# One decode step of attention plus a gated feed-forward: the score sum moved from VectorE trees to identity matmuls, and all loads moved to one queue of 4 MiB transfers

## The chip, the cores and the metric

The kernel runs on one core of one Trainium2 chip. The metric is the device time of one execution in microseconds; three runs of the kernel before took 1370.96 to 1371.06 us, with a median of 1371.04 us. One further execution was taken by the hardware profiler; its page and its trace are what the rows below come from.

## The reference

One token `x` (640 values) is normalised and goes through two branches whose results are added to it:

```python
def _A_ref(x, k_cache, v_cache, wq, wo):          # 32 heads, Sk = 32768 keys, Dh = 128
    q = (x @ wq).reshape(B, Sq, Hq, Dh).transpose(0, 2, 1, 3)
    scores = einsum("bhqd,bhkd->bhqk", q, k) * (Dh ** -0.5)
    p = softmax(scores, axis=-1)
    o = einsum("bhqk,bhkd->bhqd", p, v)
    return o.transpose(0, 2, 1, 3).reshape(B, Sq, Hq * Dh) @ wo

def _B_ref(x, w_gate, w_up, w_down):              # F = 1728
    return (silu(x @ w_gate) * (x @ w_up)) @ w_down

xn = _layernorm(x)
return x + _A_ref(xn, k_cache, v_cache, wq, wo) + _B_ref(xn, w_gate, w_up, w_down)
```

Everything is bf16. Each of the 32 heads has its own K and V of 32768 x 128 values, 8 MiB each, and each is read once: 536.9 MB of the 555.2 MB that the profiled execution moved. There is one query per head, so a key gives 128 products and one sum.

## The kernel before

**Layout.** A head's K is laid over the 128 partitions so that partition p holds keys 256p to 256p+255, each with its 128 values side by side. A score is therefore a product with the head's query (which `qb` holds, the same in all partitions) and a sum along the free axis. K and V are each cut into four chunks of 64 keys per partition (2 MiB) a head.

**Queues.** SyncE issues x, the five pieces of `wq`, then the 128 K chunks into a ring of four slots (`krings`), with the feed-forward weights after the second chunk and `wo` after the fourth. A K chunk is issued when VectorE has finished with the chunk that lay in its slot (line 510). ScalarE issues the 128 V chunks on its own queue into another ring of four slots (`vrings`), each when TensorE has finished with the chunk before it in that slot (line 403). The feed-forward weights lie in `vrings` at first, so V waits for the feed-forward part (line 405).

**VectorE, per K chunk (lines 352 to 378).** One product of 128x8192 elements in place (L361), then a tree of four in-place additions over halves of the head axis, 64, 32, 16 and 8 wide (L365), then a reduction of the last 8 (L368). Once per head follow the maximum (L343) and a reciprocal (L349).

**GpSimd** takes the maximum over the partitions (L387) and scales it (L390), and later sums the softmax denominators (L394). **ScalarE** takes the exponential (L424) and copies out the head's result (L414). **TensorE** multiplies V with the probabilities: per V chunk 64 matmuls with one column (L466), and per head two more with `wo` (L440).

**Start and end.** The feed-forward part runs near the start (L287, L328) and borrows VectorE between K chunks. The output is a row in one partition: two additions of 1x640 at the very end (L483, L485) and one store (L524).

## Time and profile before

| what | value |
|---|---|
| median of 3 runs | 1371.04 us |
| span of the profiled execution | 1367.0 us (what lies around the span is not on the page; the median is 4.0 us above it) |
| VectorE busy | 1263.9 us, 92% |
| TensorE matmuls busy | 272.6 us, 20% |
| moved by DMA | 555.19 MB, 406 GB/s over the span |

In the profile, L361 is line 361 of the kernel; a group of instructions stands with its count, its busy time and the mean time of one. "DMA share" in the view by stretches is the time that packets took as a share of 16 DMA engines; since packets overlap a little, a full stretch shows 1.00 to 1.06. "PEclk" is the granted clock of TensorE as a share of full speed. Idle time stands with what ended it.

### The profile page before, as it was taken

To read this page: it belongs to the slowest core of one execution; us is meant where nothing else is said; L and a number is where in the kernel's file an instruction comes from. 1 tells how busy PE (TensorE), PEld (TensorE's weight loads), DVE (VectorE), ACT (ScalarE), POOL (GpSimd) and SP (SyncE) were. 2 spreads that over 40 slices of the span, in tenths; PEclk is the share of its full clock that TensorE was granted. 3 is DMA by queue.
4 is the path that set the end of the run, shared out by engine and by line. 5 is a ranking of instruction groups with operands and counts; after the bars stand their busy time and mean duration, and the time that the engine had idled before them with its cause. 6 is when DMAs were issued, how large, how long until landed. Compare 5 with 4: busy or idle time off the path is not lost.

```text
span 1367.0 us, 18528 instructions
## 1 busy us (share of the span) xinstructions
PE 272.6 (20%) x8474; PEld 240.2 (18%) x8474; DVE 1263.9 (92%) x859; ACT 31.9 (2%) x102; POOL 201.3 (15%) x100
## 2 busy tenths in 40 slices
PE   3320102222111222211122221112222111222222
PEld 1220102222101222210122221112222111222222
DVE  5907999999999999999999999999999999999994
ACT  0000000000000000000000000000000000000000
POOL 0000222111111211111121111111111111110120
PEclk9555555555555555555555555555555555555555
DMA  9999599999999999999999999999999999999994
GB/s 389 401 415 381 214 424 388 419 419 415 416 426 418 427 418 422 424 419 426 418 421 420 424 420 423 427 420 425 422 421 424 417 427 425 419 426 427 414 381 183
DMA packets 44850, 555.19 MB, mean 406 GB/s; under 512 B 4258, under 2 KB 10084, under 8 KB 11364
## 3 DMA queue, kind: packets, MB, share of 16 engines
q1 hardware_dynamic: 26340, 285.57, 50.4%
q10 hardware_dynamic: 18432, 268.44, 46.5%
q8 instruction: 66, 1.08, 0.3%
q14 instruction: 12, 0.10, 0.0%
HBM read 553.99 MB, written 0.00 MB: 405 GB/s over the span
## 4 chain that ended last, share of the span: by engine, by line
DVE 90%; another core or an unknown queue 3%; issue 2%; SPq 2%; DMA 1%; PE 1%; POOL 0%; ACT 0%; POOLq 0%
DVE krings L365 43%; DVE krings L361 40%; DVE sc L368 6%; DMA vrings<-in_B_w_down_dram 1%; SPq L499 1%; PE ps L466 1%; SPq L498 0%; DVE rzb L349 0%; PE ps L287 0%; SPq L494 0%; DVE pmax L343 0%; PE ps L440 0%; SPq L513 0%; DVE rows L483 0%
## 5 line engine op out<-in xcount | busy, mean ns | idle before, releaser
L365 DVE TENSOR_TENSOR krings<-krings 128x4096 bf16<-128x4096 bf16 (+3 forms) x512 | 592.9, 1158 | 17.5
L361 DVE TENSOR_TENSOR krings<-krings,qb 128x8192 bf16<-128x8192 bf16 x128 | 564.9, 4413 | 43.5 <-DMA krings<-in_A_k_cache_dram 43.5
L466 PE MATMUL ps<-P,vrings 128*128 128x1 bf16 x8192 | 229.5, 165 | 209.0 <-ACT P L424 105.5
L466 PEld LDWEIGHTS ps<-P,vrings 128*128 128x128 bf16 x8192 | 223.9, 104 | 228.4 <-ACT P L424 105.8
L387 POOL PARTITION_ALL_REDUCE gmaxb<-pmax x32 | 136.3, 4259 | 542.6 <-DVE pmax L343 542.6
L440 PE MATMUL ps<-wqo,ocol 128*1 128x320 bf16 x64 | 22.0, 449 | 850.7 <-ACT P L424 850.7
L440 PEld LDWEIGHTS ps<-wqo,ocol 128*1 128x1 bf16 x64 | 2.8, 81 | 853.6 <-ACT P L424 853.2
L368 DVE TENSOR_REDUCE sc<-krings 128x64 f32<-128x512 bf16 x128 | 87.8, 686 | 4.4
L394 POOL PARTITION_ALL_REDUCE zb<-rowsum x32 | 40.3, 1258 | 265.2 <-issue 265.2
L390 POOL TENSOR_SCALAR negb<-gmaxb 128x1 f32<-128x1 f32 x32 | 24.6, 767 | 351.4 <-issue 351.4
L424 ACT ACTIVATE P<-sc,negb 128x256 bf16<-128x256 f32 x32 | 16.3, 508 | 917.1 <-POOL negb L390 917.1
L349 DVE RECIPROCAL rzb<-zb 128x1 f32<-128x1 f32 x32 | 4.9, 153 | 14.4 <-POOL zb L394 14.4
L414 ACT ACTIVATE ocol<-ps,rzb 128x1 bf16<-128x1 f32 x32 | 8.4, 263 | 360.4 <-PE ps L466 360.4
L274 DVE CAST qb<-ps 128x512 bf16<-128x512 f32 x8 | 5.5, 692 | 11.9 <-PE ps L264 11.9
L343 DVE TENSOR_REDUCE pmax<-sc 128x1 f32<-128x256 f32 x32 | 13.4, 419 | 1.1
L264 PE MATMUL ps<-wqo,xnb 128*128 128x512 bf16 x40 | 10.1, 418 | 7.6 <-DMA wqo<-in_A_wq_dram 7.6
L287 PE MATMUL ps<-xncol,vrings 128*128 128x1 bf16 (+1 forms) x140 | 4.4, 168 | 16.7 <-DMA vrings<-in_B_w_down_dram 16.7
L287 PEld LDWEIGHTS ps<-xncol,vrings 128*128 128x128 bf16 (+1 forms) x140 | 4.3, 108 | 17.2 <-DMA vrings<-in_B_w_down_dram 17.2
L328 PE MATMUL ps<-vrings,hcol 128*1 128x320 bf16 (+1 forms) x28 | 6.4, 400 | 0.8 <-DVE hcol L307 0.8
L264 PEld LDWEIGHTS ps<-wqo,xnb 128*128 128x128 bf16 x40 | 4.2, 106 | 13.2 <-issue 9.5
L424 ACT ACTIVATION_READ_ACCUMULATOR P<-sc,negb 128x1 f32 x32 | 6.0, 187 | 0.0
L328 PEld LDWEIGHTS ps<-vrings,hcol 128*1 128x1 bf16 (+1 forms) x28 | 2.8, 104 | 4.4 <-issue 1.1
(31 smaller groups left out, 17.1 us busy)
## 6 DMA issues: line engine op xcount, KB each, us to landing
krings<-in_A_k_cache_dram SPq DMA_DIRECT2D x128, 2048.0 KB, 17.1
vrings<-in_A_v_cache_dram ACTq DMA_DIRECT2D x128, 2048.0 KB, 26.1
wqo<-in_A_wq_dram SPq DMA_DIRECT2D x5, 1024.0 KB, 9.0
wqo<-in_A_wo_dram SPq DMA_DIRECT2D x1, 5120.0 KB, 71.2
vrings<-in_B_w_gate_dram SPq DMA_DIRECT2D x1, 2160.0 KB, 26.4
vrings<-in_B_w_up_dram SPq DMA_DIRECT2D x1, 2160.0 KB, 31.1
vrings<-in_B_w_down_dram SPq DMA_DIRECT2D x1, 2080.0 KB, 31.7
vrings<-in_B_w_down_dram SPq DMA_DIRECT2D x1, 80.0 KB, 18.1
```

The costliest lines, as they stand in the source:

```text
L264: mm = t.matmul(QPS[b], lhsT=xnb[:, c, :], rhs=wq_v[:, c, b * QB:(b + 1) * QB], start=(c == 0), stop=(c == NC_D - 1))
L343: v1 = dve_max.inc(v.tensor_reduce(out=pmax[:, b % SR:b % SR + 1], in_=scs, axis=AX.X, op=ALU.max))
L361: dve_t.inc(v.tensor_tensor(out=kr, in0=kr, in1=qbh[:, None, :].to_broadcast([128, CKK, DH]), op=ALU.mult))
L365: dve_t.inc(v.tensor_tensor(out=kr[:, :, 0:w], in0=kr[:, :, 0:w], in1=kr[:, :, w:2 * w], op=ALU.add))
L368: v3 = dve_t.inc(v.tensor_reduce(out=scs[:, c * CKK:(c + 1) * CKK], in_=kr[:, :, 0:TREE[-1]], axis=AX.X, op=ALU.add))
L387: v1 = pool_g.inc(g.partition_all_reduce(gmaxb[:, s:s + 1], pmax[:, s:s + 1], channels=128, reduce_op=ReduceOp.max))
L390: v2 = pool_neg.inc(g.tensor_scalar(out=negb[:, s:s + 1], in0=gmaxb[:, s:s + 1], scalar1=-c_scale, scalar2=None, op0=ALU.mult))
L394: v3 = pool_z.inc(g.partition_all_reduce(zb[:, s:s + 1], rowsum[:, s:s + 1], channels=128, reduce_op=ReduceOp.add))
L424: v1 = act_exp.inc(a.activation(out=P[:, b % PR, :], in_=sc[:, b % SCR, :], func=ACTF.Exp, bias=negb[:, b % SR:b % SR + 1], scale=c_scale, ...
L440: mm = t.matmul(psR[0:1, b, 0:DBW], lhsT=ocol[:, h:h + 1], rhs=wo_v[:, h, b * DBW:(b + 1) * DBW], start=(h == 0), stop=(h == H - 1))
L466: mm = t.matmul(ob[:, 0:1], lhsT=ring[:, vslot, jj * DH:(jj + 1) * DH], rhs=P[:, pslot, j:j + 1], start=(j == 0), stop=(j == NJ - 1))
L499: c_ffn.inc(sp.dma_start(wd_sb[:, 0:FB - 1, :], B_w_down[0:(FB - 1) * 128, :].rearrange("(j p) n -> p j n", p=128)))
```

## The change

The kernel is written anew around the same reference; what matters for its time is this.

**Loads.** All loads go through SyncE's queue, in one order, into one ring of six slots of 4 MiB (128 keys per partition): `wq` first (it lies in slots 4 and 5), then K and V chunks of 4 MiB in turn, V one head behind K, then the feed-forward weights (two slots), `wo` (two slots) and the last head's V, whose last chunk comes in four pieces of 64, 32, 16 and 16 keys per partition. Each load waits until its slot's owner is used up: K until TensorE has summed it, V until TensorE has multiplied it.

**Scores.** VectorE still forms the product K*q in place, 128x8192 at a time, two per chunk. The tree is gone: TensorE adds the 128 products of a key with 16 matmuls of 512 columns against an identity matrix, each taking 8 of the 128 products of 64 keys and accumulating into one PSUM bank of 64x8; VectorE then reduces the last 8 out of PSUM. Four banks take turns.

**Order on TensorE.** Per K chunk: 32 identity matmuls, then the 128 matmuls of one V chunk of the head before. The feed-forward part, the products with `wo` for 31 heads and the last head's V come after all K chunks.

**Form of the rest.** x, the normalisation, the feed-forward result and the output lie over the partitions as columns (128x5), not as a row in one partition; the products with `wo` and `w_down` use the weights as the stationary operand with one moving column, 5 matmuls per head instead of 2. The query is copied out of PSUM by ScalarE instead of VectorE. Silu is computed with the exponential. The last head is copied out by VectorE.

The diff, cut to what the prediction speaks of:

```diff
-    CKK = 64 if NJ >= 64 else NJ
-    KR = 4
-    VR = 4
-    TREE = [64, 32, 16, 8]
+    CH = 128
+    HF = 64
+    G = 512 // HF
+    SLOTS = 6
+    NBK = 4
+    TAIL = [64, 32, 16, 16]
...
+    units += [("ffn",), ("wo",)]
+    units += [("v", H - 1, c) for c in range(NCH)]
...
+            @block.sync
+            def sp(e):
+                e.dma_start(xb[:, :], A_x[0, 0:1, :].rearrange("o (p c) -> (o p) c", c=NCD)).then_inc(s_x, 16)
+                e.dma_start(wq, A_wq.rearrange("(p c) n -> p (c n)", c=NCD)).then_inc(s_wq, 16)
...
+                for u in units:
+                    s = slot_of[u]
+                    for o in ([s, s + 1] if u[0] in ("ffn", "wo") else [s]):
+                        if o in owner:
+                            e.wait_ge(*owner.pop(o))
+                    if u[0] == "k":
+                        _, h, c = u
+                        e.dma_start(ring[:, s, :], kv_src(A_k_cache, h, c * CH, CH)).then_inc(s_slot[s], 16)
+                        owner[s] = (s_qk, NHF * (h * NCH + c + 1))
...
+                        e.dma_start(wo, A_wo.rearrange("(h d) n -> d h n", d=DH)).then_inc(s_wo, 16)
...
+                def scores(k):
+                    h, c = divmod(k, NCH)
+                    kv = ring[:, slot_of[("k", h, c)], :].rearrange("p (j d) -> p j d", d=DH)
+                    for i in range(NHF):
+                        n = k * NHF + i
+                        t.wait_ge(s_mul, n + 1)
+                        if n >= NBK:
+                            t.wait_ge(s_red, n - NBK + 1)
+                        ob = bank[n % NBK].rearrange("p (j e) -> p j e", e=G)
+                        for g in range(DH // G):
+                            mm = t.matmul(ob, lhsT=ident[:, :], rhs=kv[:, i * HF:(i + 1) * HF, g * G:(g + 1) * G],
+                                          start=(g == 0), stop=(g == DH // G - 1))
+                        mm.then_inc(s_qk, 1)
...
+                for k in range(NK):
+                    scores(k)
+                    h, c = divmod(k, NCH)
+                    if h >= 1:
+                        pv(h - 1, c)
...
-                    for w in TREE:
-                        v.wait_ge(dve_t.sem, dve_t.n)
-                        dve_t.inc(v.tensor_tensor(out=kr[:, :, 0:w], in0=kr[:, :, 0:w], in1=kr[:, :, w:2 * w],
-                                                  op=ALU.add))
...
+                    for i in range(NHF):
+                        kh = kv[:, i * HF:(i + 1) * HF, :]
+                        v.tensor_tensor(out=kh, in0=kh, in1=q[:, None, :].to_broadcast([128, HF, DH]),
+                                        op=ALU.mult).then_inc(s_mul, 1)
...
+                    for i in range(NHF):
+                        n = k * NHF + i
+                        v.wait_ge(s_qk, n + 1)
+                        j = c * CH + i * HF
+                        v.tensor_reduce(out=sc[:, h % SCR, j:j + HF],
+                                        in_=bank[n % NBK].rearrange("p (j e) -> p j e", e=G),
+                                        axis=AX.X, op=ALU.add).then_inc(s_red, 1)
...
+                v.wait_ge(s_att, 1)
+                v.tensor_tensor(out=outb[:, :], in0=xf[:, :], in1=acc, op=ALU.add).then_inc(s_fin, 1)
```

How the work stands on the engines: a row is a line of the respective kernel, its operation, what it writes and reads, the shape, and in brackets what it waits for. First VectorE, in the middle of the K stream. Before, two chunks of 64 keys (kd0, kd1 are the loads, dve_t VectorE's own last result):

```order
L361 TENSOR_TENSOR krings<-krings,qb 128x8192 [waits kd0]
L365 TENSOR_TENSOR krings<-krings 128x64x64 [waits dve_t]
L365 TENSOR_TENSOR krings<-krings 128x64x32 [waits dve_t]
L365 TENSOR_TENSOR krings<-krings 128x64x16 [waits dve_t]
L365 TENSOR_TENSOR krings<-krings 128x64x8 [waits dve_t]
L368 TENSOR_REDUCE sc<-krings 128x64 [waits dve_t]
L361 TENSOR_TENSOR krings<-krings,qb 128x8192 [waits kd1]
```

Now, one head of 256 keys, that is two chunks of 128 (slot2 and slot4 are the loads, qk the identity matmuls, z the softmax denominator of the head before):

```order
L385 TENSOR_TENSOR ring<-ring,qb 128x8192 [waits slot2,act_q]
L385 TENSOR_TENSOR ring<-ring,qb 128x8192
L393 TENSOR_REDUCE sc<-ps 128x64 [waits qk] x2
L385 TENSOR_TENSOR ring<-ring,qb 128x8192 [waits slot4,act_q]
L385 TENSOR_TENSOR ring<-ring,qb 128x8192
L393 TENSOR_REDUCE sc<-ps 128x64 [waits qk] x2
L400 TENSOR_REDUCE pmax<-sc 128x1 [waits red,gm]
L373 RECIPROCAL rzb<-zb 128x1 [waits z]
```

The four additions between a product and its reduction are gone, and between the products and the reductions VectorE now waits for TensorE. TensorE at the same place, before (vd0, vd1 are V loads):

```order
L440 MATMUL ps<-wqo,ocol 1x320 [waits c_wo,act_ov,act_exp]
L440 MATMUL ps<-wqo,ocol 1x320
L466 MATMUL ps<-P,vrings 128x1 [waits vd0]
L466 MATMUL ps<-P,vrings 128x1 x63
L466 MATMUL ps<-P,vrings 128x1 [waits vd1]
L466 MATMUL ps<-P,vrings 128x1 x63
```

and now (mul are VectorE's products, red its reductions, exp the exponential, ov the copy of a head's result):

```order
L241 MATMUL ps<-ring,ident 128x512 [waits red,mul]
L241 MATMUL ps<-ring,ident 128x512 x15
L241 MATMUL ps<-ring,ident 128x512 [waits red,mul]
L241 MATMUL ps<-ring,ident 128x512 x15
L263 MATMUL ps<-P,ring 128x1 [waits slot5,ov,exp]
L263 MATMUL ps<-P,ring 128x1 x127
L241 MATMUL ps<-ring,ident 128x512 [waits red,mul]
```

The 32 identity matmuls of a K chunk now stand ahead of each V chunk's 128 matmuls on the same engine, and the next chunk's identity matmuls behind them. Last, the end of SyncE's queue, which before held K chunks only and then the store:

```order
L166 DMA ring<-in_A_k_cache_dram 128x16384 [waits qk]
L176 DMA ring<-in_A_v_cache_dram 128x16384 [waits pv]
L179 DMA ring<-in_B_w_gate_dram 128x8640 [waits pv,qk]
L180 DMA ring<-in_B_w_up_dram 128x8640
L181 DMA ring<-in_B_w_down_dram 128x13x640
L183 DMA ring<-in_B_w_down_dram 64x640
L185 DMA ring<-in_A_wo_dram 128x32x640 [waits pv,qk]
L176 DMA ring<-in_A_v_cache_dram 128x16384 [waits qk]
L171 DMA ring<-in_A_v_cache_dram 128x8192 [waits pv]
L171 DMA ring<-in_A_v_cache_dram 128x4096
L171 DMA ring<-in_A_v_cache_dram 128x2048 x2
L187 DMA out_0_dram<-outb 128x5 [waits fin]
```

The feed-forward weights and `wo` moved from the start of the queue to a place behind the last K chunk, and the last head's V stands behind them.

More of the change, by code (lines that the diff above doesn't have):

```diff
@@ L90, in bass_parallel_sum__gqa_block_cached__swiglu_ffn__decode_kernel @@
-    for q in range(NVC):
-        _emit_v(q)
-    assert CKV == CKK, "V-in-K-slot staging needs equal chunk sizes"
-    LASTV_Q0 = (H - 1) * NCV
-    def v_buf(q):
-        return ("v", q % VR, None)
-    WO_POS = min(KR - 1, NKC - 1)
-    FFNW_POS = min(1, NKC - 1)
+    units = []
+    for h in range(H):
+        for c in range(NCH):
+            units.append(("k", h, c))
+            if h >= 1:
+                units.append(("v", h - 1, c))
+    units += [("ffn",), ("wo",)]
+    units += [("v", H - 1, c) for c in range(NCH)]
@@ L105, in sem @@
             return es.enter_context(nc.semaphore(name))
[L107 to L112 removed]
+        ring = sbt("ring", [128, SLOTS, CE], BF16)
+        qb = sbt("qb", [128, H * DH], BF16)
         sc = sbt("sc", [128, SCR, NJ], F32)
         P = sbt("P", [128, PR, NJ], BF16)
[L115 removed]
```

699 lines of the change are left out of this document (288 added, 411 removed).

## The prediction

> **What bounds the kernel now.** I read the page's shares and chain first, then who waited for whom, then the stretches of the span, then one chunk in order of time.
>
> ```profile
> span 1367.0 us, 18528 instructions
> PE 272.6 (20%) x8474; PEld 240.2 (18%) x8474; DVE 1263.9 (92%) x859; ACT 31.9 (2%) x102; POOL 201.3 (15%) x100
> DVE 90%; another core or an unknown queue 3%; issue 2%; SPq 2%; DMA 1%; PE 1%; POOL 0%; ACT 0%; POOLq 0%
> L365 DVE TENSOR_TENSOR krings<-krings 128x4096 bf16<-128x4096 bf16 (+3 forms) x512 | 592.9, 1158 | 17.5
> L361 DVE TENSOR_TENSOR krings<-krings,qb 128x8192 bf16<-128x8192 bf16 x128 | 564.9, 4413 | 43.5 <-DMA krings<-in_A_k_cache_dram 43.5
> L368 DVE TENSOR_REDUCE sc<-krings 128x64 f32<-128x512 bf16 x128 | 87.8, 686 | 4.4
> DMA packets 44850, 555.19 MB, mean 406 GB/s; under 512 B 4258, under 2 KB 10084, under 8 KB 11364
> SPq L513 <- DVE sc L368: 1196.7, 121, 31.2
> ```
>
> VectorE is busy for 92% of the span and makes up 90% of the chain that ended last. It waited for a K load once, for 43.5 us, while K's queue waited for VectorE 121 times. Two groups carry it: the product (564.9 us) and the tree (592.9 us). One chunk in order of time, with the head's end behind it:
>
> ```profile
> 1295.42 0.69 DVE L368 TENSOR_REDUCE sc<-krings 128x64 f32<-128x512 bf16 x1
> 1296.02 4.42 DVE L361 TENSOR_TENSOR krings<-krings,qb 128x8192 bf16<-128x8192 bf16 x1
> 1300.47 4.74 DVE L365 TENSOR_TENSOR krings<-krings 128x4096 bf16<-128x4096 bf16 x4
> 1305.24 0.69 DVE L368 TENSOR_REDUCE sc<-krings 128x64 f32<-128x512 bf16 x1
> 1305.96 0.42 DVE L343 TENSOR_REDUCE pmax<-sc 128x1 f32<-128x256 f32 x1
> 1306.37 4.41 DVE L361 TENSOR_TENSOR krings<-krings,qb 128x8192 bf16<-128x8192 bf16 x1
> ```
>
> From reduction to reduction a chunk takes 1305.24 - 1295.42 = 9.82 us, and a head's end adds (1306.37 - 1296.02) - 9.82 = 0.53. 128 x 9.82 + 32 x 0.53 = 1274 us, of a span of 1367. Per head VectorE needs 4 x 9.82 + 0.53 = 39.8 us for 16.78 MB of K and V, which is 421 GB/s. The second question is therefore how far the DMA engines could go:
>
> ```profile
> 0.00:5.00 5.00, 0.00 (x0) 0.00 (x0) 2.88 (x8) 1.28 (x1) 0.19 (x4) 1.00 0.50 184
> 10.00:15.00 5.00, 0.00 (x0) 0.00 (x0) 0.00 (x0) 0.00 (x0) 0.00 (x0) 1.00 1.02 431
> 15.00:20.00 5.00, 3.93 (x13) 1.53 (x14) 0.95 (x2) 0.00 (x0) 0.00 (x0) 1.00 1.01 433
> 25.00:30.00 5.00, 1.18 (x6) 0.33 (x4) 4.44 (x3) 0.00 (x0) 0.00 (x0) 0.90 1.02 417
> 50.00:60.00 10.00, 4.62 (x22) 1.91 (x20) 9.83 (x7) 1.28 (x1) 0.00 (x0) 0.84 1.02 372
> 140.00:160.00 20.00, 0.00 (x0) 0.00 (x0) 19.66 (x14) 0.00 (x0) 4.52 (x1) 0.50 0.55 210
> 180.00:200.00 20.00, 0.00 (x0) 0.00 (x0) 19.62 (x15) 0.00 (x0) 4.52 (x1) 0.50 1.01 429
> 210.00:215.00 5.00, 5.00 (x192) 5.00 (x192) 4.93 (x4) 0.00 (x0) 0.56 (x1) 0.50 0.50 170
> 200.00:1300.00 1100.00, 218.82 (x7224) 198.59 (x7224) 1080.20 (x718) 24.24 (x84) 176.26 (x83) 0.50 1.00 421
> 1340.00:1350.00 10.00, 0.00 (x0) 0.00 (x0) 6.05 (x8) 0.00 (x0) 0.37 (x1) 0.50 0.75 318
> 1350.00:1360.00 10.00, 5.07 (x168) 4.53 (x169) 0.00 (x0) 0.75 (x3) 0.26 (x1) 0.50 0.01 2
> ```
>
> The last three columns are TensorE's clock, DMA share and GB/s. Full stretches give 417 to 433; the average of 421 holds dips such as 210:215, when V's queue ran dry. So the two limits lie close together, and removing VectorE's can gain only what the DMA engines lost: the half-empty stretch around 140:160, the dips, and the last 20 us, in which almost nothing was loaded.
>
> **The change part by part.** *The tree leaves VectorE*: 592.9 us of busy time. What stays is 128 products of 4.41 (565 us), 128 reductions out of PSUM, and the heads' ends (17). The reduction's nearest rows are L368, 0.69 us for 512 elements from SBUF, and the copy of as many out of PSUM:
>
> ```profile
> L274 DVE CAST qb<-ps 128x512 bf16<-128x512 f32 x8 | 5.5, 692 | 11.9 <-PE ps L264 11.9
> 17.73 0.15 PEld L264 LDWEIGHTS ps<-wqo,xnb 128*128 128x128 bf16 x1 [0.28 <-issue]
> 18.16 0.15 PEld L264 LDWEIGHTS ps<-wqo,xnb 128*128 128x128 bf16 x1 [0.28 <-issue]
> 18.90 6.79 PEld L264 LDWEIGHTS ps<-wqo,xnb 128*128 128x128 bf16 x32 [0.16 <-issue]
> 48.17 6.45 PE L328 MATMUL ps<-vrings,hcol 128*1 128x320 bf16 x28 [0.84 <-DVE hcol L307]
> 608.09 5.28 PE L466 MATMUL ps<-P,vrings 128*128 128x1 bf16 x192
> ```
>
> Both say 0.69; 128 x 0.69 = 88. VectorE comes to 670 us of work and is no bound by itself.
>
> *TensorE gains 4096 identity matmuls of 512 columns.* The 512-column matmuls of the query start 0.43 us apart at first (17.73, 18.16) and then 6.79 / 32 = 0.212 us apart. The granted clock stood at 0.50 all through the one-column matmuls (200:1300) and rose to a mean of 0.84 in 50:60, around the 28 matmuls of 320 columns. So each chunk's identity matmuls should begin at 0.43 and reach 0.212 within some 3 us: about 7 x 0.43 + 25 x 0.212 = 8.3 us; bounds 6.8 (all fast) and 13.8 (all slow). The 128 V matmuls take 128 x 5.28 / 192 = 3.5 us, as before.
>
> *The new waits.* In a chunk VectorE waits for the matmuls and the next products queue behind that wait. Loop = first product 4.42 + matmuls + one reduction 0.69 + hops between engines about 0.3 + half a head's end 0.26 = 5.7 + 8.3 = 14.0 us, bounds 12.5 and 19.5. The second product hides under the first half's matmuls, the V matmuls under the next product (3.5 against 4.4). The loads that it must keep pace with are a K and a V chunk, 8.39 MB: 19.6 us at 428 GB/s. So VectorE should wait for loads about 5 us a chunk; even the slow bound only just fills that time.
>
> TensorE also waits for the exponential ahead of a head's first V chunk, with the next identity matmuls behind it. That chain is GpSimd's:
>
> ```profile
> 1323.06 0.51 ACT L424 ACTIVATE P<-sc,negb 128x256 bf16<-128x256 f32 x1 [25.10 <-POOL negb L390]
> 1346.29 0.37 POOL L387 PARTITION_ALL_REDUCE gmaxb<-pmax  x1 [13.28 <-DVE pmax L343]
> 1354.28 0.51 ACT L424 ACTIVATE P<-sc,negb 128x256 bf16<-128x256 f32 x1 [21.87 <-POOL negb L390]
> 1365.42 0.26 SPq L524 DMA_DIRECT2D out_dram<-outb  x1
> 2.00 0.48 DVE L205 CAST rows<-xrowb 1x640 f32<-1x640 bf16 x1 [1.16 <-DMA xrowb<-in_A_x_dram]
> ```
>
> It took 1323.06 - 1305.96 = 17 us beside a busy VectorE and 8 us (1346.29 to 1354.28) beside an idle one. After a head's maximum the next K chunk lands about 5 us later and its matmuls end 13 us after that: 18 us, so the exponential is there. Cost 0; if the cover went it would be a few us a head, out of the same 5 us per chunk of spare time.
>
> *The ring.* A slot is needed again five transfers (49 us) after its data landed; K is used up in 14 us, V in about 20. SyncE's wait for a slot, with every later load behind it, should never empty the queue. At the start `wq` holds two slots until about 27 us (5.24 MB at 428 plus the start's loss, then matmuls for 10 us) while 16.8 MB of loads queue ahead: cost 0.
>
> *The bytes.* They are nearly the same, and now set the end. The rate: one queue alone gave 431 and 433 (10:20, rows of 8 KB and then others), two queues 429 (180:200). I take 428; bounds 421 (the average, dips and all) and 433. `wo` and `w_down`, 7.45 MB in rows of 1280 bytes, were in flight when a full stretch gave 372 (50:60): I take that. So (555.19 - 7.45) MB / 428 = 1279.8 us and 7.45 / 372 = 20.0 us.
>
> [...]
>
> *Start.* In 0:5 the core moved 0.92 MB, worth 2.15 us at 428: 2.85 us lost, and the order of the first two loads is the same.
>
> *End.* Before, 20.7 us ran from GpSimd's taking up the last head's maximum (1346.29) to the end of the span (1367.0). Now the maximum is long past; behind the last byte come its landing (about 1.2, as between issue and use of x at 2.00), 16 V matmuls (0.6), VectorE's copy, 5 matmuls, one addition of 128x5 (together about 1.2 with hops) and the store (1367.0 - 1365.42 = 1.6): about 5 us. The feed-forward matmuls and 155 with `wo` lie under the last two V chunks (19.6 us): 155 x 27 ns = 4 us if they run like L466, 16 us if each takes its whole weight load of about 0.1 us. Cost 0, bound 4.
>
> Sum: 2.85 + 1279.8 + 20.0 + 5 = 1307.7 us of span; with the 4.0 us between the profiled span and the median, **1312 us**. At 421 it is 1333, at 433 1297.
>
> **The rivals.**
>
> *The rate is not kept by one queue.* Between two transfers of one queue an engine might idle, where a second queue fills in. Against it: 431 and 433 with SyncE's queue alone; for it: 417 in 25:30, also one queue, with narrower rows. At 415 the time is 1320 + 32 = 1352, and from about 410 nothing is gained (1368): still faster, or equal.
>
> *The identity matmuls become the bound.* Their moving operand is 64 runs of 8 values, 256 bytes apart; no row before shows such a read, all were contiguous. If a matmul takes m, the loop is 5.7 + 32m, and it passes 19.6 us at m = 0.43. The time is then 25 (first K) + 64 x loop + 29 (last two V chunks, the end, 4.0): 1371 at m = 0.464, from which the change is slower; at 0.86, half the slow rate, 1371 becomes about 2180. For it: at m = 0.43, the slow clock throughout, there is no room left. Against it: 8 values side by side leave the read dense, and bursts of 320 columns did raise the clock.
>
> [...]
>
> *No change.* m near 0.46, or a rate near 409: both need a coincidence, 1368 to 1374.
>
> *The change does less than it says.* If VectorE's reduction out of PSUM or its waits took twice what I say, the loop grows by 1 us of 5 spare: no effect.
>
> **How the numbers follow.** A difference of 0.2% (2.7 us) is about what a measurement of this kernel can tell from none. Forecast, bound by loads at 421 to 433: 0.72, 1297 to 1333. A lower rate of one queue: 0.10, 1333 to 1365. Above 433: 0.03. No change: 0.04. Identity matmuls as the bound: 0.11, 1375 to 2200. Faster 0.72 + 0.10 + 0.03 = 0.85, same 0.04, slower 0.11. The range leaves out the slower and equal cases and what lies above 433, together 0.18: 1296 to 1355.
>
> **What would show it.** Right: DMA share near 1.00 in every stretch from 5 us to the last 10, 425 to 433 GB/s; VectorE near 50% busy and its idle time ended by K loads; identity matmuls near 0.43 and then 0.21 us apart, and a clock above 0.50 in the mean; K's and V's queue waiting for slots without emptying; about 5 us between the last load and the end. Wrong: VectorE's idle time ended by TensorE with the DMA share below 0.9 (the second rival), or loads that never stop but at under 418 GB/s (the first).

## The result, and the profile after

The changed kernel takes **1325.53 us** (median of four runs, 1325.38 to 1326.16) against 1371.05 us: a ratio of 0.9671, with a 95% interval of 0.9657 to 0.9684. That is faster by 45.5 us, and 13.5 us slower than the forecast of 1312. The profiled execution has a span of 1323.6 us.

First the page of the changed kernel: shares, the chain that ended last, and the costliest groups (L241 is the identity matmul, L385 the product, L393 the reduction out of PSUM, L263 the V matmul, L202, L205 and L210 GpSimd's three operations of a head).

```profile
span 1323.6 us, 22586 instructions
...
PE 821.4 (62%) x10654; PEld 464.3 (35%) x10654; DVE 668.2 (50%) x341; ACT 31.6 (2%) x108; POOL 92.0 (7%) x102
...
DMA packets 25548, 555.45 MB, mean 420 GB/s; under 512 B 2480, under 2 KB 8304, under 8 KB 8560
...
q8 instruction: 84, 1.38, 0.4%
...
DMA 68%; PE 16%; DVE 8%; SPq 4%; issue 3%; POOL 1%; ACT 0%; DVEq 0%; POOLq 0%
...
L241 PE MATMUL ps<-ring,ident 128*128 128x512 bf16 x2048 | 588.4, 459 | 450.7 <-DVE ring L385 450.7
L385 DVE TENSOR_TENSOR ring<-ring,qb 128x8192 bf16<-128x8192 bf16 x128 | 560.6, 4422 | 322.1 <-DMA ring<-in_A_k_cache_dram 322.1
```

The chain that was 90% VectorE is now 68% loads. VectorE has 668.2 us of work, and the 322.1 us that it stood idle before its products were ended by K loads. One chunk in order of time, from the timeline (start, duration, instruction, and in brackets the idle time before it and what ended it):

```profile
702.38 8.76 DVE L385 TENSOR_TENSOR ring<-ring,qb 128x8192 bf16<-128x8192 bf16 x2 [6.16 <-DMA ring<-in_A_k_cache_dram]
706.86 8.82 PE L241 MATMUL ps<-ring,ident 128*128 128x512 bf16 x32 [8.19 <-DVE ring L385]
712.26 0.69 DVE L393 TENSOR_REDUCE sc<-ps 128x64 f32<-128x512 f32 x1 [1.13 <-PE ps L241]
...
715.72 0.69 DVE L393 TENSOR_REDUCE sc<-ps 128x64 f32<-128x512 f32 x1 [2.76 <-PE ps L241]
716.51 0.42 DVE L400 TENSOR_REDUCE pmax<-sc 128x1 f32<-128x256 f32 x1
721.78 4.43 DVE L385 TENSOR_TENSOR ring<-ring,qb 128x8192 bf16<-128x8192 bf16 x1 [4.79 <-DMA ring<-in_A_k_cache_dram]
```

The 32 identity matmuls take 8.82 us (9.2 in the mean: 588.4 us over 64 chunks), the chunk's own work lasts from 702.38 to 716.9, and then VectorE waits 4.79 us for the next K chunk. Up to here the changed kernel does what was forecast. The missing time is in the stretches of the span (the last three columns are TensorE's clock, the DMA share and GB/s):

```profile
0.00:5.00 5.00, 1.17 (x4) 1.00 (x4) 1.05 (x7) 1.28 (x1) 0.39 (x5) 1.00 0.77 254
100.00:200.00 100.00, 63.36 (x808) 35.25 (x807) 51.70 (x24) 2.25 (x9) 8.31 (x8) 0.73 1.01 429
600.00:700.00 100.00, 62.71 (x800) 34.94 (x800) 51.70 (x24) 2.25 (x9) 6.57 (x8) 0.71 1.00 427
1250.00:1260.00 10.00, 4.72 (x136) 3.84 (x133) 1.92 (x2) 0.00 (x0) 0.40 (x1) 0.83 0.90 362
1260.00:1270.00 10.00, 6.74 (x24) 2.76 (x25) 8.23 (x3) 0.00 (x0) 0.00 (x0) 0.66 0.73 295
1270.00:1280.00 10.00, 5.25 (x138) 4.10 (x136) 1.18 (x3) 0.00 (x0) 0.37 (x1) 0.85 0.36 131
1280.00:1290.00 10.00, 4.43 (x140) 4.31 (x140) 0.00 (x0) 0.98 (x5) 0.26 (x1) 0.50 1.06 367
```

In the loop the loads run at 427 to 429 GB/s, as forecast. Then they run dry: against 428 GB/s the three stretches from 1250 to 1280 lack (66 + 133 + 297) x 10 / 428 = 11.6 us. SyncE's own timeline shows an issue that took 38.64 us just there (L183 is the short remainder of `w_down`):

```profile
1237.41 1.36 SPq L181 DMA_DIRECT2D ring<-in_B_w_down_dram  x1
1238.81 38.64 SPq L183 DMA_DIRECT2D ring<-in_B_w_down_dram  x1
1277.55 0.53 SPq L185 DMA_DIRECT2D ring<-in_A_wo_dram  x1
```

That was the first theory: a held queue. A second came from the landings. The trace has 16 increments of the semaphore for each of these loads, and the page counts 16 DMA engines; I read one increment as one engine that has done its part, which no row shows by itself. By that reading the spread between the first and the last increment of one load is how far the engines have drifted apart. It grew steadily: 1.7 us at 46, 8.7 at 325, 16.3 at 722, 28.7 at 1259 (each at the time of the last increment). In the kernel before, loads that landed at about the last three of these times had spreads of 1.5 and 3.6, 4.5 and 5.4, 7.6 and 9.2 us (two loads each), where VectorE set the pace, K's queue waited for it for 1196.7 us in all, and the engines had time to catch up; in e6 below, where TensorE sets the pace, the spread stays under 4 us from 100 us on. The kernel uses a load after its 16th increment (the product at 702.38 began 0.10 us after the one at 702.28), that is, by the same reading, when its slowest engine is done, and at 1259 the 16 engines were 14.0 us behind the first in the mean: the slowest was 14.7 us behind that.

### The profile page after: what moved, and what is told of

It reads as the page before. It is cut to its first block, busy times and chain, and to the rows that moved or that the text cites. A ratio compares the mean times of both kernels' runs of the same rounds, so it can differ in the third digit from the quotient of the medians.

```text
span 1323.6 us, 22586 instructions
## 1 busy us (share of the span) xinstructions
PE 821.4 (62%) x10654; PEld 464.3 (35%) x10654; DVE 668.2 (50%) x341; ACT 31.6 (2%) x108; POOL 92.0 (7%) x102
## 4 chain that ended last, share of the span: by engine, by line
DMA 68%; PE 16%; DVE 8%; SPq 4%; issue 3%; POOL 1%; ACT 0%; DVEq 0%; POOLq 0%
DMA ring<-in_A_k_cache_dram 68%; PE ps L241 16%; DVE ring L385 7%; SPq L183 3%; SPq L176 1%; PE ps L263 1%; POOL gmax L202 0%; POOL negb L205 0%; SPq L171 0%; DVE sc L393 0%; SPq L181 0%; ACT P L329 0%; SPq L185 0%; DVE pmax L400 0%; DVEq L381 0%
## 5 line engine op out<-in xcount | busy, mean ns | idle before, releaser
L241 PE MATMUL ps<-ring,ident 128*128 128x512 bf16 x2048 | 588.4, 459 | 450.7 <-DVE ring L385 450.7
L385 DVE TENSOR_TENSOR ring<-ring,qb 128x8192 bf16<-128x8192 bf16 x128 | 560.6, 4422 | 322.1 <-DMA ring<-in_A_k_cache_dram 322.1
L241 PEld LDWEIGHTS ps<-ring,ident 128*128 128x128 bf16 x2048 | 228.7, 114 | 785.6 <-DVE ring L385 452.8
L393 DVE TENSOR_REDUCE sc<-ps 128x64 f32<-128x512 f32 x128 | 88.5, 692 | 277.0 <-PE ps L241 277.0
L263 PEld LDWEIGHTS ps<-P,ring 128*128 128x128 bf16 x8192 | 216.4, 97 | 30.8 <-ACT P L329 10.6
L263 PE MATMUL ps<-P,ring 128*128 128x1 bf16 x8192 | 216.4, 163 | 15.5 <-ACT P L329 9.6
L205 POOL TENSOR_SCALAR negb<-gmax 128x1 f32<-128x1 f32 x32 | 58.5, 1829 | 358.3 <-issue 358.3
L202 POOL PARTITION_ALL_REDUCE gmax<-pmax x32 | 20.0, 624 | 537.7 <-DVE pmax L400 537.7
L329 ACT ACTIVATE P<-sc,negb 128x256 bf16<-128x256 f32 x32 | 16.2, 508 | 1231.8 <-POOL negb L205 1231.8
L210 POOL PARTITION_ALL_REDUCE zb<-rsum x32 | 12.8, 400 | 295.3 <-issue 295.3
L225 PE MATMUL ps<-ring,xnb 128*128 128x512 bf16 x40 | 11.1, 446 | 11.4 <-DMA ring<-in_A_wq_dram 11.4
L225 PEld LDWEIGHTS ps<-ring,xnb 128*128 128x128 bf16 x40 | 4.4, 112 | 17.6 <-issue 14.5
## 6 DMA issues: line engine op xcount, KB each, us to landing
ring<-in_A_k_cache_dram SPq DMA_DIRECT2D x64, 4096.0 KB, 45.5
```

The source lines that it names most:

```text
L202: g.partition_all_reduce(gmax[:, s:s + 1], pmax[:, s:s + 1], channels=128, reduce_op=ReduceOp.max).then_inc(s_g, 1)
L205: g.tensor_scalar(out=negb[:, s:s + 1], in0=gmax[:, s:s + 1], scalar1=-c_scale, scalar2=None, op0=ALU.mult).then_inc(s_neg, 1)
L225: mm = t.matmul(bank[b], lhsT=xnb[:, c, :], rhs=wq_v[:, c, b * 512:(b + 1) * 512], start=(c == 0), stop=(c == NCD - 1))
L241: mm = t.matmul(ob, lhsT=ident[:, :], rhs=kv[:, i * HF:(i + 1) * HF, g * G:(g + 1) * G], start=(g == 0), stop=(g == DH // G - 1))
L263: mm = t.matmul(O[h % 2], lhsT=ring[:, s, j * DH:(j + 1) * DH], rhs=P[:, h % PR, jj:jj + 1], start=(jj == 0), stop=(jj == NJ - 1))
L329: a.activation(out=P[:, h % PR, :], in_=sc[:, h % SCR, :], func=ACTF.Exp, bias=negb[:, h % SR:h % SR + 1], scale=c_scale, accum_out=rsum[: ...
```

## The experiments

The landings of one K or V load at about 1238 us, sorted into the first four engines, the next eight and the last four, are the measure for all runs that follow: means of the groups, in us behind the first engine, with the last engine in brackets, the packets of the page's queue q8 (kind "instruction"), and the median time. The groups go by the order of landing, since the trace does not number the engines. This table is worked out from the increments in the traces (the row of before is a K load):

```
kernel                             first 4  next 8  last 4 (last)   q8   time
before                               0.0      0.4     2.8  (5.6)    66  1371.05
changed                              0.5     14.3    25.4 (27.5)    84  1325.53
e1  long rows of w_down, wo          0.5     14.6    26.1 (27.8)    84  1322.80
e2  half of the V matmuls            0.5      8.8    25.4 (26.9)    52  1325.16
e3  V matmuls issued twice           0.7     25.7    27.1 (28.6)   146  1327.81
e4  wide V product                   0.4      6.3    26.0 (27.3)    38  1325.25
e5  VectorE's tree kept              0.1      1.2     4.1  (7.6)    67  1347.81
e6  identity matmuls doubled         0.1      0.2     1.4  (2.9)   100  1436.85
e7  no reductions on GpSimd          0.3      8.3    15.9 (16.2)    85  1313.03
e8  e4 and e7 together               0.1      4.1     7.3  (8.2)    39  1304.44
e9  a third reduction on GpSimd      0.5     14.4    26.0 (27.9)    84  1325.73
e10 e8, w_down in long rows          0.2      4.3     7.5  (8.4)    40  1332.69
e11 multiplication to ScalarE        0.5      8.3    15.6 (15.9)    83  1313.52
e12 e4 and e11 together              0.6      4.4     6.8  (7.7)    38  1304.01
```

In e7 and e11 there are only two groups left, eight engines at 0 to 5 us and eight at 14 to 16.

**e1, long rows.** `w_down` and `wo` are loaded as long contiguous rows instead of rows of 1280 bytes; the products with them are then not the reference's.

```diff
-  e.dma_start(wd[:, 0:FB - 1, :], B_w_down[0:(FB - 1) * 128, :].rearrange("(j p) n -> p j n", p=128))...
-  e.dma_start(wd[0:FL, FB - 1, :], B_w_down[(FB - 1) * 128:F, :])...
+  e.dma_start(flat[:, f0 + 2 * NCD * F:f0 + 2 * NCD * F + F * D // 128], <w_down, F * D / 128 values a partition>)...
-  e.dma_start(wo, A_wo.rearrange("(h d) n -> d h n", d=DH))...
+  e.dma_start(flat[:, WO_S * CE:WO_S * CE + H * D], A_wo.rearrange("(p x) n -> p (x n)", p=128))...
```

> Edit: w_down and wo are loaded as long contiguous rows (17 and 40 KB per partition) instead of rows of 1280 bytes, same bytes, same order, same waits; the weights then lie in another arrangement, so the two products that use them are not the reference's. Theory 'held queue': SyncE's queue stood 38.6 us in the issue of the second w_down load because the 1280-byte rows before it filled the queue, and the DMA engines ran dry meanwhile (1256 to 1278); without those rows the dry stretch is gone and, with 2.9 us for the better rate of long rows (7.45 MB at 428 instead of 367), the time falls by 13 to 15 us, to 1311 (1308 to 1314). Theory 'slowest engine': one or a few of the 16 DMA engines fall behind all through the run and never run dry, so they set the end whatever the others do; the dry stretch is the others' waiting. Then only the better rate counts: 1322 (1320 to 1324).

Measured: 1322.80 us, ratio 0.9654 (0.9639 to 0.9668). SyncE was no longer held, and the dry stretch went, but the loss only moved to the end. SyncE's timeline of e1 (L184 is `wo`):

```profile
1254.52 0.33 SPq L184 DMA_DIRECT2D ring<-in_A_wo_dram  x1
```

The stretches of e1:

```profile
1270.00:1280.00 10.00, 4.76 (x136) 3.84 (x133) 1.18 (x3) 0.00 (x0) 0.37 (x1) 0.81 0.94 386
1290.00:1300.00 10.00, 3.35 (x79) 3.32 (x80) 0.99 (x9) 0.00 (x0) 0.40 (x1) 0.50 0.81 342
1300.00:1310.00 10.00, 9.48 (x278) 9.40 (x276) 0.00 (x0) 0.00 (x0) 0.00 (x0) 0.50 0.34 141
1310.00:1320.00 10.00, 4.48 (x136) 4.01 (x133) 0.39 (x2) 0.00 (x0) 0.00 (x0) 0.50 0.12 42
```

The engines still lay 22 us apart at 1306. The held queue by itself is worth at most these 2.7 us. That left the drift as the cause to be tested, and the question became what delays which engine.

**e2, e3 and e4, instruction fetches.** The page counts packets of kind "instruction" (q8, "fetches" in what follows) apart. The three runs change TensorE's number of V matmuls, and with it the number of these packets: e2 leaves every second one out (half of the V product is missing), e3 issues each twice, the second time into an unused PSUM column, and e4 takes four columns of P as the stationary operand and moves 512 columns of V, then adds the four parts by four small matmuls (and leaves the identity matmuls three PSUM banks instead of four).

```diff
 e2   -  for _ in range(n):                          +  for _ in range(n // 2):       (j += 2)
 e3   +  if h < H - 1:  for j in range(CH):  t.matmul(misc[:, 100:101], lhsT=ring[...], rhs=P[...])
 e4   -  t.matmul(O[h % 2], lhsT=ring[:, s, j * DH:(j + 1) * DH], rhs=P[:, h % PR, jj:jj + 1], ...)
      +  t.matmul(bank[4 + h % 2][0:4, :], lhsT=P[:, h % PR, jj:jj + 4], rhs=ring[:, s, j * DH:(j + 4) * DH], ...)
```

> Edit: every second V matmul is left out (4096 fewer matmuls, 8192 fewer TensorE instructions), all loads unchanged; the weighted sum over V then takes only half of the keys. Theory 'slowest engine', with instruction fetches as what sets engines back: fetched packets fall from 84 to about 52, the spread between first and last engine at the last K load from 28.7 us to about 17, and the time by about 10 us, to 1315 (1312 to 1319). Theory 'held queue': TensorE is not on the path and the queue is held as before: 1325 (1323 to 1327).

> Edit: each V chunk's 128 matmuls are issued a second time into an unused PSUM column (7936 more matmuls, 15872 more instructions); loads and results unchanged. The loop grows to about 16.6 us of the 19.6 us that the loads give it, so TensorE should not become the bound. Theory 'slowest engine' with fetches as the cause: about 62 more fetched packets, spread near 49 us, time up by about 20 us, to 1345 (1338 to 1352). Theory 'held queue': 1326 (1324 to 1329).

> Edit: for 31 heads the probabilities are the stationary operand, 4 columns at a time, and V the moving one, 512 columns: 32 matmuls per chunk instead of 128; the four diagonal blocks are turned into a column by 4 small matmuls per head. About 5900 fewer matmuls, some 11800 fewer instructions. Theory 'slowest engine' with fetches as the cause: about 38 fetched packets instead of 84, spread near 13 us, time 1310 (1306 to 1315), which beats both kernels. Theory 'held queue': 1325 (1323 to 1328). If the 512-column V matmuls stall the loop (8.3 + 6.9 us of TensorE per chunk, loop 16.5 us) it would be slower than 1330, with VectorE's idle time ended by TensorE.

Measured: 1325.16, 1327.81 and 1325.25 us, ratios 0.9672 (0.9656 to 0.9688), 0.9690 (0.9676 to 0.9705) and 0.9670 (0.9656 to 0.9684). As the cause of the missing time the fetches by themselves fall: 1315, 1345 and 1310 us were expected by that theory, and going from 84 of them to 38 gained 0.3 us. But the table splits them off cleanly. The lag of the middle eight engines follows the packets (6.3, 8.8, 14.3 and 25.7 us for 38, 52, 84 and 146), while the last four stay at 25 to 27 whatever TensorE does. These four set the end, and something else delays them. The single packets point to it. Of the 32 KB packets of the changed kernel between 100 and 1200 us, 189 took over 1.25 times the median of 1.21 us ("long" below). 107 of them ran within 0.5 us of an instruction packet. Of the other 82, 63 ran while GpSimd stood in "issue" ahead of a head's multiplication (L205) and 16 while it stood so ahead of the sum (L210).

**e5, the tree kept.** Ring, queue, transfers and end are the new ones, but VectorE sums as before.

```diff
-  scores(k)                                                       # TensorE's identity matmuls
+  for l, w in enumerate([64, 32, 16, 8]):                         # VectorE, on each half behind its product
+      v.tensor_tensor(out=kh[:, :, 0:w], in0=kh[:, :, 0:w], in1=kh[:, :, w:2 * w], op=ALU.add)
+  v.tensor_reduce(out=sc[...], in_=kh[:, :, 0:8], axis=AX.X, op=ALU.add)
```

> Everything of the changed kernel but the identity matmuls: VectorE sums K*q by four halving additions and one reduction again, as before the change; ring, single queue, 4 MiB loads and the end stay new. Theory (both kernels stand close to the same limit of loads; the matmuls only remove VectorE as the bound): VectorE's loop is 128 x 9.82 + 32 x 0.53 = 1274 us from the first K at about 25 us, so it ends near 1299; the last two V chunks wait for the slots of the last K, 8.4 MB at 428 = 20 us, and the end is 5 us: span 1324 to 1330, time about 1331. So nearly the whole gain of 45 us would come from the loads and the end, and about 5 us from the matmuls. Rival (the 592.9 us taken off VectorE are what gained): the time stays near 1371.

Measured: 1347.81 us, ratio 0.9835 (0.9818 to 0.9851), half way: 23.2 us of the 45.5 come with the loads and the new end, and 22.3 with the matmuls. VectorE's loop was nearly as expected (it ends at 1302.6 us, 1299 was worked out), the end was not. The timeline from the last head's maximum:

```profile
1302.23 0.42 DVE L401 TENSOR_REDUCE pmax<-sc 128x1 f32<-128x256 f32 x1
...
1302.75 0.37 POOL L202 PARTITION_ALL_REDUCE gmax<-pmax  x1 [13.34 <-DVE pmax L401]
1314.64 0.26 POOL L205 TENSOR_SCALAR negb<-gmax 128x1 f32<-128x1 f32 x1 [11.52 <-issue]
1324.74 0.40 POOL L210 PARTITION_ALL_REDUCE zb<-rsum  x1 [9.84 <-issue]
...
1329.31 6.36 PE L293 MATMUL ps<-ocol,ring 128*128 128x1 bf16 x155
...
1335.53 6.97 PE L263 MATMUL ps<-P,ring 128*128 128x1 bf16 x256
```

With no spare time on VectorE the last maximum comes at 1302 instead of 45 us ahead of the last load (1273.2 and 1318.7 in the changed kernel), and GpSimd's 22 us, the `wo` matmuls and all V matmuls of the last two chunks, which had lain under loads, stand in a row. By the expectation's own sum an end under the loads would have given about 1331, so some 17 of the 22.3 us are the uncovered end: the matmuls gain less by what they take off the loop than by letting the end overlap. The "issue" of 11.52 and 9.84 us ahead of operations of 0.26 and 0.40 us is the row that later gave the cause away.

**e6, identity matmuls doubled.** Each half's 16 are issued twice. The second pass begins with `start` again and so sums anew: other than the expectation says, the scores stay as they are and only the matmuls are doubled.

```diff
-  for g in range(DH // G):
+  for g in list(range(DH // G)) * 2:
```

> Each half's 16 identity matmuls are issued twice (scores come out doubled, so the output is not the reference's). Theory (the loop is 5.7 us plus 32 matmuls' starts, and only above 19.6 us does it set the time): now 64 starts a chunk, 7 at 0.43 and 57 at 0.21 us: 15.1 us, loop 20.8 us, over the 19.6 us that the loads of a chunk take. Time 25 + 64 x 20.8 + 29 = 1385 us (1360 to 1420), VectorE's idle time ended by TensorE rather than by K loads. Rival (the matmuls hide beside the products, so that the loop is the larger of the two and not their sum): 15.1 us stays below 19.6, time unchanged at 1326.

Measured: 1436.85 us, ratio 1.0484 (1.0468 to 1.0500), slower than before. VectorE's idle time is now ended by TensorE, and K loads end 19.5 us of it instead of 322.1 (the view of waits: total us, times, longest):

```profile
DVE sc L393 <- PE ps L241: 703.6, 128, 6.2
...
DVE ring L385 <- DMA ring<-in_A_k_cache_dram: 19.5, 1, 19.5
```

The last row of two heads in VectorE's timeline of e6:

```profile
708.58 0.42 DVE L400 TENSOR_REDUCE pmax<-sc 128x1 f32<-128x256 f32 x1
...
750.23 0.42 DVE L400 TENSOR_REDUCE pmax<-sc 128x1 f32<-128x256 f32 x1
```

A head takes 750.23 - 708.58 = 41.65 us, 20.8 a chunk, as worked out; every other head takes 43.7. The loop is the sum of its parts, not the larger of them, and the rival that the matmuls hide beside the products falls. The expectation was still 52 us low: 34 us for the longer heads (64 x 0.53) and 16 for the end, which is uncovered as in e5 (45 us from the last maximum, not 29).

**e7 and e8, no reductions on GpSimd.** Maximum and sum over the partitions go to TensorE (a matmul with the identity, one with a row of ones, one with the matrix of ones) and VectorE; e8 adds the wide V product.

```diff
-  g.partition_all_reduce(gmax[...], pmax[...], reduce_op=max);  g.tensor_scalar(out=negb, in0=gmax, scalar1=-c_scale);
-  g.partition_all_reduce(zb[...], rsum[...], reduce_op=add)
+  t.matmul(row, lhsT=pmax[:, s:s + 1], rhs=ident);  v.tensor_reduce(out=gmax[0:1, z:z + 1], in_=row, op=ALU.max)
+  t.matmul(peak, lhsT=ones[0:1, :], rhs=gmax[0:1, s:s + 1]);  v.tensor_scalar(out=negb, in0=peak, scalar1=-c_scale)
+  t.matmul(tot[s], lhsT=ones, rhs=rsum[:, s:s + 1])
```

> GpSimd's two reductions over the partitions per head (maximum and sum) are done by TensorE and VectorE instead; GpSimd is idle in the loop. Theory (GpSimd's reductions hold back the four DMA engines that are 25 to 28.7 us behind the first at 1258 us, instruction fetches the eight that are 13 to 15 behind): the last group closes up to the others, the spread at the end of the stream is about 13 to 15 us instead of 28.7, and the time falls by about as much: 1311 us. Rival (these four engines are slow by themselves or by another traffic): spread 25 to 29 us and 1325 us, unchanged.

> As the run without GpSimd's reductions, with the V product in its wide form too (P as the stationary operand, 512 columns of V moving), which needs half the instructions and so half the fetches. Theory (GpSimd's reductions slow four engines, fetches eight): no group is more than 6 to 8 us behind, and the time is that of 16 engines that all move 32 KB in 1.21 us, 432 GB/s: about 1304 us (1301 to 1309), faster than the changed kernel by 1.6%. Rival (neither sets the end): 1325 us.

Measured: **1313.03 us** (ratio 0.9580, 0.9566 to 0.9594) and **1304.44 us** (0.9518, 0.9504 to 0.9532), 2.0 and 0.4 us from the expectations. Without GpSimd's reductions the group of four late engines is gone and the first group counts eight; then the engines whose lag follows the fetches set the end (16.2 us with 85 of them in e7), and with fewer fetches it moves again (8.2 us with 39 in e8). GpSimd is the cause of the last group's lag, but these runs do not say which of its operations.

**e9, a third reduction.** GpSimd reduces a constant column in addition, behind the sum of each head.

```diff
+  g.partition_all_reduce(spare[:, :], ones[:, 0:1], channels=128, reduce_op=ReduceOp.max)
```

> The changed kernel with a third reduction over the partitions per head on GpSimd (the maximum of a constant column into a spare one, used by nobody). Theory (each reduction holds back the last four DMA engines by a fixed amount, about 0.4 us of their 25 to 28.7 us over 64 reductions): with 96 reductions the last four are 37 to 43 us behind the first by 1260 us, the other twelve as before (0 to 16), and the time grows by 12 to 14 us to 1338 us (1333 to 1344). GpSimd would be occupied some 34 us of the 39 of a head, so the exponential is still in time. Rival (what gained without GpSimd's reductions was the earlier exponential, or something else that came with it): spread 25 to 29 us and 1325 to 1327 us.

Measured: 1325.73 us, ratio 0.9676 (0.9663 to 0.9689), and the last four at 26.0 us: nothing changed. The theory that each reduction delays the engines falls. GpSimd's timeline shows why, and what is left:

```profile
717.43 0.35 POOL L204 PARTITION_ALL_REDUCE gmax<-pmax  x1 [15.40 <-DVE pmax L405]
729.08 2.19 POOL L207 TENSOR_SCALAR negb<-gmax 128x1 f32<-128x1 f32 x1 [11.30 <-issue]
739.33 0.40 POOL L212 PARTITION_ALL_REDUCE zb<-rsum  x1 [8.06 <-issue]
739.65 0.44 POOL L215 PARTITION_ALL_REDUCE spare<-ones  x1
```

The added reduction (L215) followed the sum's at once. Only where GpSimd changes from a reduction to the multiplication, or back, does it stand for 8 to 11 us in "issue" here.

**e11 and e12, the multiplication to ScalarE.** Both reductions stay on GpSimd; only the maximum times -c, one value a partition, moves. e12 adds the wide V product.

```diff
-  g.tensor_scalar(out=negb[:, s:s + 1], in0=gmax[:, s:s + 1], scalar1=-c_scale, scalar2=None, op0=ALU.mult)
+  a.activation(out=negb[:, h % SR:h % SR + 1], in_=gmax[:, h % SR:h % SR + 1], func=ACTF.Copy, scale=-c_scale)
```

> The changed kernel with both of GpSimd's reductions kept and only the small multiplication between them (the maximum times -c, one element a partition) moved from GpSimd to ScalarE. Theory (what holds back the last four DMA engines is not a reduction but GpSimd's change from one kind of operation to the other, some 8 to 12 us of issue time twice a head in which it fetches code; the third reduction of the run before, right behind another, cost neither time nor spread): without the multiplication GpSimd never changes over, its issue time before the second reduction falls from about 9 us to under 2, the last four engines close up to the fetch group, spread about 15 us instead of 28 at 1260 us, 1313 us (1311 to 1315) as without any GpSimd work. Rival (the reductions themselves do it, whatever stands between them): 1325 us and a spread of 25 to 29.

> The wide V product with that multiplication on ScalarE, both reductions still on GpSimd. Theory (change-overs of GpSimd and instruction fetches of TensorE are all that separates the engines): spread 6 to 8 us, 1304 to 1306 us, as without GpSimd's reductions (1304.4). Rival (the reductions themselves): 1325 us.

Measured: **1313.52 us** (ratio 0.9588, 0.9574 to 0.9602) and **1304.01 us** (0.9518, 0.9504 to 0.9532). GpSimd's timeline of e11:

```profile
710.29 0.35 POOL L202 PARTITION_ALL_REDUCE gmax<-pmax  x1 [39.06 <-DVE rzb L373]
711.60 0.39 POOL L207 PARTITION_ALL_REDUCE zb<-rsum  x1 [0.96 <-ACT P L329]
748.42 0.35 POOL L202 PARTITION_ALL_REDUCE gmax<-pmax  x1 [36.44 <-DVE rzb L373]
```

The same of the changed kernel, and from its view of waits what TensorE's V matmuls waited for the exponential:

```profile
717.03 0.37 POOL L202 PARTITION_ALL_REDUCE gmax<-pmax  x1 [16.95 <-DVE pmax L400]
728.67 1.98 POOL L205 TENSOR_SCALAR negb<-gmax 128x1 f32<-128x1 f32 x1 [11.27 <-issue]
739.91 0.40 POOL L210 PARTITION_ALL_REDUCE zb<-rsum  x1 [9.27 <-issue]
```

```profile
PE ps L263 <- ACT P L329: 9.6, 2, 5.9
```

From the maximum to the sum it now takes 1.3 us instead of 22.9, and the group of four late engines is gone. It is the change-over, not the reduction. Nor is it the multiplication's own run: 63 of the 82 long packets of the changed kernel ran before it began, and in e11 4 long packets are left away from instruction packets. That the exponential comes earlier in e11 is no rival either: in the changed kernel TensorE waited for it twice, at 75 and 105 us, 9.6 us in all, while the loads went on. The two causes together, in the stretches of e12:

```profile
100.00:200.00 100.00, 80.23 (x337) 31.15 (x335) 52.10 (x26) 3.94 (x14) 2.20 (x6) 0.91 1.00 431
...
1250.00:1260.00 10.00, 7.56 (x35) 2.70 (x33) 1.34 (x4) 1.54 (x5) 0.73 (x2) 0.99 0.94 352
1260.00:1270.00 10.00, 4.90 (x152) 4.77 (x153) 0.93 (x8) 0.23 (x2) 0.00 (x0) 0.50 1.07 358
```

SyncE's timeline of e12 (L186 is the remainder of `w_down`):

```profile
1219.01 36.89 SPq L186 DMA_DIRECT2D ring<-in_B_w_down_dram  x1
```

The DMA share of e12 is 0.94 and more in each of these stretches, although SyncE is held for 36.89 us at the same place: with the engines 7.7 us apart instead of 27.5 the held queue did not starve them. (In e11, still 16 us apart, the share falls to 0.81 and 0.71 from 1250 to 1270, with SyncE held for 37.78 us.) e12 is the fastest version here, 4.8% below the kernel before and 21.5 us below the changed one.

**e10, `w_down` in long rows.** e8 with the hidden index laid out so that 108 partitions each load 16 neighbouring rows of `w_down` as one, and gate and up take every 16th column as weights.

```diff
+  e.dma_start(wd[0:FP, :, :], B_w_down.rearrange("(p j) n -> p j n", j=FB))          # FB = 16, FP = 108
-  lhsT=w[:, c, j * 128:j * 128 + n]
+  lhsT=w[:, c, :].rearrange("p (a b) -> p a b", b=FB)[:, :, j]
```

> As the run with the wide V product and without GpSimd's reductions, with the feed-forward's hidden index laid out so that 108 partitions each load 16 neighbouring rows of w_down as one row of 20 KB (gate and up take every 16th column as weights); the result is the reference's. Theory (with the engines in step, what is left is SyncE's 30.9 us at the issue of w_down's remainder, during which the queue runs thin: 323 and 360 GB/s in 1250:1260 and 1260:1270, worth 4.1 us at 431): 1301 us (1300 to 1302.5). Rival (the narrow rows of wo, which stay, set these stretches): 1304.

Measured: 1332.69 us, ratio 0.9726 (0.9712 to 0.9739), 28 us worse than e8: a miss by my own edit, in two ways. Row of TensorE's timeline and of the view of its line, of e8:

```profile
1264.03 4.13 PE L315 MATMUL ps<-xn,ring 128*128 128x1 bf16 x140 [1.62 <-DMA ring<-in_B_w_down_dram]
```

```profile
L315 PEld LDWEIGHTS ps<-xn,ring x140: 95/96/157, 1264.0 to 1267.9; 128*128 128x128 bf16 x130, 128*64 128x64 bf16 x10
```

The same of e10, and one of its stretches:

```profile
1278.10 32.37 PE L312 MATMUL ps<-xn,ring 128*108 128x1 bf16 x160 [14.72 <-DMA ring<-in_B_w_down_dram]
```

```profile
L312 PEld LDWEIGHTS ps<-xn,ring x160: 275/298/301, 1278.1 to 1310.1; 128*108 128x108 bf16 x160
```

```profile
1260.00:1270.00 10.00, 3.39 (x17) 1.32 (x14) 0.17 (x1) 0.68 (x1) 0.00 (x0) 0.91 1.01 200
```

Weights of every 16th column load in 298 ns instead of 96, and a matmul follows the next after 0.202 us (32.37 / 160) instead of 0.030; the 32 us no longer fit under the last loads, and all that TensorE has still to do comes behind them. The load over 108 partitions came with 12 increments (44 for gate, up and down together instead of 48, with one jump at the issue), which I read as 12 engines; its 20 KB packets took 1.46 us where 32 KB took 1.22, and the stretch above moved 200 GB/s. So this run does not tell whether the held queue of e8 still costs anything; it stays open. The thin stretches of e12 are worth at most (79 + 73) x 10 / 431 = 3.5 us.

## Why the prediction was right, and where it was wrong

- **What bounds the kernel before, and what can be gained.** Right. VectorE with its tree set the time, and the two limits lay close: with VectorE's tree kept, e5 gains only half.
- **VectorE's remaining work.** Right: 668.2 us against 670, 692 ns for a reduction out of PSUM against 0.69.
- **The identity matmuls.** Right: 8.82 us a chunk against 8.3, loop 14.5 with the head's end against 14.0, and 4.79 us of waiting for loads against about 5. The granted clock rose to 0.71 to 0.73 in the loop. The number 4096 ahead of the working is a slip: the kernel issues 2048 (64 chunks of 32, L241 x2048), and the working itself goes by 32 a chunk. The reads in runs of 8 values ran like contiguous ones: 64 in 15.40 us in the quickest chunks of e6, which is 7 at 0.43 us and 57 at 0.217, where the query's contiguous ones had 0.212. The rival that they become the bound needed twice as many of them (e6); its formula for the loop held there, but its 29 us behind the last maximum was 16 too low, since GpSimd's work then stands in the open.
- **"The ring ... should never empty the queue".** Wrong in place: it did not empty in the loop, but from 1250 to 1280 the DMA share fell to 0.36. The narrow rows themselves ran at 367 GB/s against 372.
- **Start and end.** Near. 254 GB/s in the first 5 us lost (428 - 254) x 5 / 428 = 2.0 us against 2.85. From the last landing at 1318.7 to the end of the span it took 4.9 us, where the forecast's 5 had 1.2 of landing in it.
- **The bytes: the step that failed.** The sum took (555.19 - 7.45) MB / 428 as if the stream ended when the mean of the engines had moved that much. The rate itself was right (427 to 429), but the stream ended with its slowest engine, and that was 14.7 us behind the mean at 1259 us. This is where the missing time lies: with the change-overs of GpSimd gone (e11) the time is 1313.52, with half of the fetches gone too (e12) 1304.01. The latter is 8 us under the forecast, since with both gone the rate is 431 as well.
- **The 4.0 us between the span and the median.** Wrong, and by luck it hid part of the miss. In the changed kernel the median is 1.9 us above the span (1325.53 and 1323.6), and in the executions of the kernel before that were timed beside e1 it is 1.8 to 1.9 as well (1371.19 us with a span of 1369.4). By that the profiled execution of the kernel before was some 2 us quicker than the median. From span to span the forecast was 15.9 us too low (1307.7 against 1323.6), not 13.5.
- **"Cost 0" for the exponential's chain on GpSimd.** Right for the wait, wrong for the price. The exponential was in time, and GpSimd's waits in that chain cost 12.0 us (1325.53 - 1313.52) through four DMA engines. The trace before already had GpSimd's idle time, and its packets could have shown that it touches the loads: of the 16 KB packets between 100 and 1200 us, 512 took over 1.25 times the median of 0.61 us; 373 of these ran away from any instruction packet, and 312 of the 373 in GpSimd's two waits in "issue", in which half of all packets ran. It did not set the time there: VectorE did, and the spread was no more than 7.6 and 9.2 us at 1256 us.
- **"The rate is not kept by one queue".** Its price was near (1325 lies between 1312 and 1352), but that is chance, as its mechanism did not hold: e12 keeps 431 GB/s with one queue.

## What to carry to other kernels

Once loads set the end, work out the end from the slowest DMA engine, not from GB/s: look at the spread between the first and the last increment of one load, early and late, and at whether it grows (here from 1.7 us at 46 to 28.7 at 1259). What an engine costs is not only what waits for it: here fewer, wider matmuls were worth 9.5 us (from e11 to e12) and a GpSimd that does one kind of thing 12.0 us (from the changed kernel to e11), with the last increment of the load at about 1238 us 27.5 us behind the first in the changed kernel, 15.9 in e11 and 7.7 in e12. In e5 and e6 the end that had lain under the loads came out into the open when the loop had no time to spare (some 17 and 16 us), so a rival that slows the loop must be priced with the end uncovered.

## What the runs showed of the hardware

In the changed kernel GpSimd stood in "issue" for 7.3 to 12.7 us each time it changed between a partition reduction and the multiplication (358.3 us ahead of 32 multiplications and 295.3 ahead of 32 sums, 11.2 and 9.2 us in the mean, twice a head):

```profile
POOL negb L205 <- issue: 358.3, 32, 12.7
POOL zb L210 <- issue: 295.3, 32, 11.2
```

Between two reductions in a row, the sum and the added one of e9, it stood for 0.0 us (32 heads):

```profile
L215 POOL PARTITION_ALL_REDUCE spare<-ones x32 | 14.1, 442 | 0.0
```

With the change-overs four of the 16 increments of a load came 25.4 us behind the first in the mean after 31 heads; without them (e11) the last increment came after 15.9 us. What GpSimd does in these waits, and how it reaches the loads, is not shown: that it fetches code, as the expectation of e11 has it, was my guess, and the trace does not number the engines.

The instruction packets are small (84 of 16 KB in the changed kernel, 0.4% of the DMA time), yet eight of the engines fall behind by 0.16 to 0.18 us for each of them (25.7 / 146, 14.3 / 84, 8.8 / 52, 6.3 / 38). Why those eight is open, and so is why the load of e10 over 108 partitions came with 12 increments.
